# One fused two-layer attention kernel: the whole replay table (order of all queues, engines, slots, extra waits) replaced by another

## The chip, the cores and the metric

The kernel runs on one core of one Trainium2 chip. The metric is the device time of one execution in microseconds (us), the median of three runs. Five engines work in parallel, each through its own queue in order: TensorE (PE: matmuls; its weight loads are shown as PEld), VectorE (DVE), ScalarE (ACT), GpSimd (POOL) and SyncE (SP, which here only issues DMAs). ACT issues some DMAs too.

## The reference

Two layers, each an attention block A and a linear-attention block B, on x of 2048 tokens by 512 in bfloat16. Both layers use the same weights, 32 heads of 16 features.

```python
x = A_x
x = x + _A_ref(_layernorm(x), A_wq, A_wk, A_wv, A_wo, A_beta)
x = x + _B_ref(_layernorm(x), B_wqkv, B_w_phi, B_wo)
x = x + _A_ref(_layernorm(x), ...)     # the same again
x = x + _B_ref(_layernorm(x), ...)
# A: 4 segments of 512 tokens; per segment
p = softmax(q k^T * scale + causal mask);  a_dot = p v
a_mem = phi(q) M / (phi(q) z + 1e-6)       # M, z: running sums over the segments before
o = sigmoid(beta) * a_mem + (1 - sigmoid(beta)) * a_dot
M, z = M + phi(k)^T v, z + sum(phi(k))
# B: over all 2048 tokens
phi_q = [softmax(q w_phi), softmax(-q w_phi)];  phi_k the same from k
o = (phi_q (phi_k^T v)) / (phi_q sum(phi_k) + 1e-6)
```

## The kernel before

The kernel is written as a list of some 3400 small operations (`Program.add`), each with the tiles it reads and writes, the engines that may run it, and a name. It works through the four segments of layer 0 and then of layer 1. In a segment s: layernorm of its four 128-token tiles (`ln`: L801 statistics, L817 the normalised xn), a transpose of xn (on PE at the start, L601, else by a DMA transpose on SP, L585), projections to K, Q and V (`a_proj`), the scores of 32 heads in blocks (`a_att`: PE writes 128x1024 score blocks to PSUM, ACT takes their exponential into a tile PT, L1104; DVE or POOL multiplies the odd diagonal blocks by a mask into D, L1110; POOL masks the even ones in place, L1113; PE multiplies PT and D by V), normalisation, output projection and residual sum, and then the same tokens' keys and queries of block B. Almost all matmuls are recorded at one helper line, L520.

Nothing of this text decides when an operation runs. Four tables do, and `replay` turns them into queues:

- `ORDER` lists all operations by number. Each is appended in that order to the queue of its engine, so the table fixes the order in each of the five queues. A number over 10000 pairs a score block with the one in front of it, so that their matmuls alternate.
- A negative number in `ORDER` stands for idle matmuls, which multiply a tile `warm` of zeros into an unused part of a PSUM bank (L1431; -401 means 25 of them, bank 0) and give no result.
- `ENGINE` has one letter for each operation that several engines could run (a, d, p, s for ACT, DVE, POOL, SP).
- `SLOTS` says which buffer of its pool, or which PSUM banks, each tile gets. `AFTER` has pairs (x, y): operation x also waits until y is done.

```python
for n, x in enumerate(ORDER):
    if x < 0:
        f = self.idle_op((-1 - x) // 16, (-1 - x) % 16)
        ...
    self.queues[op.on].append(op.i)
...
for x, y in AFTER:
    ops[x].need.add(y)
```

`finalize` then writes each queue with the semaphore waits that the data, the reuse of slots and `AFTER` ask for. An engine whose next instruction waits does nothing else meanwhile. At the start DMAs load X (tiles 0 to 3 by single 128-token tiles of 128 KB, the other twelve by groups of four, 512 KB), the weights WA_k, WA_q, WA_v in halves of 256 KB (one half on SP, one on ACT), beta (8 KB, a copy to each partition) and, all on SP, WB_v, the raw block-B weights for k and q (into tiles EQ), WA_o and w_phi, and WB_o.

Of the kernel before, what the change touches and what calls it, by code (L numbers as in the profile page):

```python
# [33 lines left out]
    0, 20, 26, 1, 23, 21, 22, 2, 3, 24, 25, 28, 4, 5, 33, 81, 27, 6, 7, 82, 8, 9, 10, 11, 53, 16, 54, 18, 55, 60, 56, 17, 57, 12, 61, -401, 62, 63,  # L34
    29, 58, 64, 65, 59, 67, 83, 84, 66, 74, 85, 89, 34, 86, 68, 103, 69, 70, 104, 87, 30, 90, 88, 105, 115, 91, 92, 116, 75, 31, 106, 93, 96, 102,
    117, 71, 97, 94, 107, 76, 157, 95, 98, 72, 110, 158, -22, 209, 73, 177, 346, 121, 122, 210, 344, 133, 347, 178, 345, 335, -33, 166, 10161, 348,
    123, 349, 337, 162, 134, 32, 351, 108, 350, 37, 124, 163, 159, 135, 352, 99, 167, 77, 1138, 109, 130, 164, 160, 125, 338, 336, 165, 118, 1131,
    111, 339, 128, -19, 182, 1140, 340, 127, 100, 168, 183, 131, 341, 342, 112, 101, 343, 180, -83, 214, 184, 113, 119, 215, 179, 78, 404, 389, 114,
    13, 79, 185, 40, 120, 193, 10198, 14, 80, 132, 405, 45, 425, 194, 145, 136, 1129, 137, 126, 199, 148, 46, 47, 169, 138, 48, 1139, 49, 129, 146,
    406, 186, 50, 51, 354, 139, 353, 746, 181, 149, 147, 140, 52, 170, 355, 755, 142, 187, 188, 143, 356, 189, 190, 200, 171, 15, 150, 144, 172, 195,  # L40
    232, 10230, 191, 426, 359, 151, 201, 196, 753, 233, 380, 202, 152, 436, 381, 36, 231, 192, 197, 173, 174, 212, 368, 211, 382, 216, 203, 213, 175,
    204, 205, 141, 206, 217, 176, -17, 219, 218, 383, 1130, 234, 10239, 207, 1141, 371, 220, 208, 1142, 221, 240, 222, 384, 369, 1143, 223, 386, 224,
    235, 407, 747, 225, 385, 263, 242, 258, 370, 387, 264, 237, 1132, 744, 248, 357, 362, 236, 259, 388, 363, 1145, 422, 238, 249, 427, 756, 745,
    261, 423, 241, 41, 153, 424, 246, 10244, 1133, 360, 260, 372, 245, 361, 226, 748, 154, 1134, 364, 247, 250, 243, 227, 228, 251, 262, 446, 373,
    266, 437, 229, 365, 252, 374, 253, 448, 428, 377, 268, 10270, 375, 447, 449, 38, 432, 429, 450, 269, 254, 451, 430, 255, 378, 431, 453, 287, 271,
    452, 440, 438, 433, 454, 288, 366, 272, 439, 390, 19, 367, 273, 434, 290, 441, 294, 391, 376, 435, 295, 282, 749, 256, 39, 276, 283, 392, 277,
    358, 442, 754, 265, 274, 257, 393, 395, 464, 289, 275, 443, 267, 465, 379, 475, 466, 285, 396, 298, 10296, 467, 397, 408, 1135, 297, 476, 468,
    42, 472, 299, 278, 1144, 279, 43, 1136, 409, 478, 284, 1137, 469, 292, 477, 286, 306, 293, 280, 473, 479, 281, 398, 1146, 470, 307, 311, 474,
    757, 399, 758, 410, 300, 301, 312, 400, 291, 411, 483, 480, 308, 316, 413, 320, 414, 317, 760, 302, 309, 484, 481, 310, 303, 321, 415, 318, 314,
    485, 416, 319, 313, 417, 759, 322, 418, 315, 304, 324, 761, 751, 323, 325, 412, 305, 571, 420, 471, 566, 750, 419, 326, 155, 752, 401, 327, 44,  # L50
    556, 572, 328, 329, 402, 330, -33, 558, 567, 156, 403, 587, 10582, 559, 421, 588, 557, 545, 816, 574, 813, 573, 583, 546, 831, 569, 547, 562,
    10564, 584, 771, 565, 568, 772, 394, 832, 589, 563, 798, 762, 331, 590, 773, 814, 585, 774, 332, 586, 333, 815, 455, 591, 833, 614, 10619, 334,
    570, 550, 620, 763, 575, 457, 764, 780, 615, 777, 456, 458, 765, 459, 778, 460, 551, 554, 768, 641, 603, 779, 462, 548, 461, 642, 592, 795, 549,
    463, 593, 796, 555, 604, 617, 598, 797, 766, 576, 616, 594, 599, 552, 769, 577, 444, 553, 618, 595, 445, 646, 770, 639, 600, 647, 596, 781, 606,
    578, 601, 597, 579, 624, 640, 580, 637, 605, 602, 581, 486, 621, 638, 487, 607, 608, 622, 609, 775, 625, 623, 489, 610, 611, 643, 653, 10651,
    488, 648, 612, 626, 627, 654, 613, 490, 497, 628, 498, 629, 652, 807, 561, 630, 808, 644, 491, 500, 657, 10655, 631, 499, 494, 645, 492, 632,
    658, 495, 776, 493, 505, 482, 496, 501, 656, 670, 782, 671, 649, 506, 502, 650, 659, 660, 809, 1192, 503, 661, 783, 673, 665, 811, 810, 679, 507,
# [1418 lines left out]
```

## Time and profile before

| | |
|---|---|
| median of 3 runs | 480.14 us (479.97 to 481.0) |
| the profiled execution's span, first to last instruction | 479.8 us |
| mean granted TensorE clock | 1.000 |
| instructions in the profile | 19249 |
| HBM read, written | 6.32 MB, 2.10 MB |

The profiled execution's span is 0.34 us under the median. A "busy" engine in the page has an instruction in flight; matmuls overlap, and so do other engines' instructions at their edges, which is why a group's busy time is less than its count times its mean. The chain that ended last is followed back from the last instruction, at each step to what released it.

### The profile page before, as it was taken

The numbers are of one execution on the slowest core, as the hardware profiler recorded it, in microseconds if no ns is written. First come the engines' busy times: TensorE is split into PE (matmuls) and PEld (weight loads), VectorE is DVE, ScalarE is ACT, GpSimd is POOL, SyncE is SP. The second block draws the span as 40 slices with busy tenths as digits, with TensorE's granted clock in tenths as the row PEclk, the third lists the DMA queues.
The fourth block names the chain that finished last, engine by engine and source line by source line (L and its number), as shares of the span: only waits on it lengthen the run. The fifth ranks groups of instructions, "written<-read, shape, count | busy, mean of one in ns | idle before, by whom it ended". The sixth has DMA issues, their size and how long they took to land.

```text
span 479.8 us, 19249 instructions
## 1 busy us (share of the span) xinstructions
PE 464.4 (97%) x8324; PEld 320.1 (67%) x8324; DVE 428.1 (89%) x1021; ACT 430.7 (90%) x668; POOL 261.0 (54%) x420
## 2 busy tenths in 40 slices
PE   8999989999999999999999999999999999999997
PEld 7776667667856567557687666766865657665763
DVE  6999999989998988599999899999998879978785
ACT  3999999999999999986799899899999999999743
POOL 3577657646756576410246485784776578761100
PEclk9999999999999999999999999999999999999999
DMA  8978752225411232232257407236145112402376
GB/s 264 160 196 132 127 78 46 46 48 78 59 23 25 46 68 47 19 39 47 55 88 93 62 9 124 58 53 81 39 56 89 25 25 48 76 19 55 69 128 187
DMA packets 115091, 35.86 MB, mean 75 GB/s; under 512 B 106816, under 2 KB 115008, under 8 KB 115008
## 3 DMA queue, kind: packets, MB, share of 16 engines
q1 hardware_dynamic: 113184, 33.06, 39.9%
q10 hardware_dynamic: 1824, 1.58, 1.0%
q8 instruction: 65, 1.06, 0.9%
q14 instruction: 18, 0.15, 0.1%
HBM read 6.32 MB, written 2.10 MB: 18 GB/s over the span
## 4 chain that ended last, share of the span: by engine, by line
PE 40%; DVE 25%; ACT 22%; DMA 8%; POOL 3%; issue 1%; POOLq 0%; DVEq 0%
PE PS L520 38%; ACT PT L1104 16%; DVE stats L801 4%; DMA OT<-O 3%; ACT Ek L1200 3%; DVE xn L817 2%; DVE X L1165 2%; DMA EQ<-xn 2%; POOL PT L1113 2%; DVE Vt L1228 1%; DVE D L1110 1%; DMA xA<-xn 1%; DMA xB<-xn 1%; PE PS L1431 1%; DVE O L1139 1%
## 5 line engine op out<-in xcount | busy, mean ns | idle before, releaser
L1104 ACT ACTIVATE PT<-PS 128x1024 bf16<-128x1024 f32 x288 | 282.4, 1068 | 6.5 <-PE PS L520 5.6
L1110 POOL TENSOR_TENSOR D<-PT,modd 128x256 bf16<-128x256 bf16 x127 | 87.2, 697 | 41.7 <-ACT PT L1104 29.5
L1113 POOL TENSOR_SCALAR_AFFINE_SELECT PT<-PT 128x512 bf16<-128x512 bf16 x128 | 83.2, 658 | 48.1 <-DVE D L1110 43.3
L520 PEld LDWEIGHTS PS<-VT,PT 128*128 128x128 bf16 x2048 | 74.7, 96 | 18.7 <-POOL PT L1113 3.8
L520 PE MATMUL PS<-VT,PT 128*128 128x17 bf16 x2048 | 81.7, 171 | 1.5 <-POOL PT L1113 0.6
L520 PE MATMUL PS<-QT,K 32*128 32x64 bf16 (+2 forms) x2176 | 74.8, 213 | 1.1 <-ACT PT L1104 0.6
L520 PE MATMUL PS<-VT,D 128*128 128x17 bf16 x512 | 59.8, 170 | 0.0
L520 PEld LDWEIGHTS PS<-QT,K 32*128 32x128 bf16 x2176 | 40.4, 93 | 20.3 <-ACT PT L1104 10.0
L1110 DVE TENSOR_TENSOR D<-PT,modd 128x256 bf16<-128x256 bf16 x129 | 45.1, 364 | 2.1 <-ACT PT L1104 2.0
L520 PEld LDWEIGHTS PS<-VT,D 128*128 128x128 bf16 x512 | 43.2, 96 | 0.0
L1228 DVE TENSOR_TENSOR Vt<-PS,Zk 128x1024 bf16<-128x1024 f32 (+1 forms) x34 | 38.9, 1159 | 1.1 <-ACT Zk L1216 0.6
L801 DVE BATCH_NORM_STATS2 stats<-X 128x6 f32<-128x512 bf16 x56 | 37.6, 683 | 1.1 <-DMA X<-in_A_x_dram 0.7
L1200 ACT ACTIVATE Ek<-PS 128x512 bf16<-128x512 f32 x64 | 36.8, 648 | 1.6 <-PE PS L520 1.4
L1207 POOL TENSOR_TENSOR Vt<-Ek 128x512 f32<-128x512 bf16 x24 | 28.2, 1175 | 17.4 <-ACT Ek L1200 15.1
L520 PE MATMUL PS<-WA_k,xA 128*128 128x256 bf16 x256 | 36.6, 273 | 0.8 <-DVE xA L907 0.5
L1165 DVE TENSOR_TENSOR X<-X,PS 128x512 bf16<-128x512 bf16 x50 | 33.5, 678 | 4.3 <-PE PS L520 4.0
L1304 POOL COPY O<-rho 128x512 bf16<-128x512 bf16 x26 | 16.2, 642 | 38.7 <-DVE rho L1297 35.4
L520 PE MATMUL PS<-xA,WA_q 128*128 128x128 bf16 x512 | 36.4, 219 | 0.7 <-DMA xA<-xn 0.5
L520 PE MATMUL PS<-WA_v,xA 128*128 128x256 bf16 x256 | 36.3, 273 | 0.3 <-DMA xA<-xn 0.3
L520 PE MATMUL PS<-WA_o,OT 128*128 128x512 bf16 x128 | 32.1, 380 | 1.3 <-DMA OT<-O 0.7
L520 PEld LDWEIGHTS PS<-xA,WA_q 128*128 128x128 bf16 x512 | 30.0, 98 | 4.8 <-issue 1.0
L817 DVE TENSOR_SCALAR xn<-X,mv,rstd 128x512 bf16<-128x512 bf16 x64 | 28.6, 466 | 4.1 <-POOL rstd L813 1.7
(158 smaller groups left out, 983.5 us busy)
## 6 DMA issues: line engine op xcount, KB each, us to landing
X<-in_A_x_dram SPq DMA_DIRECT2D x3, 512.0 KB, 11.7
out_dram<-X SPq DMA_DIRECT2D x12, 128.0 KB, 1.8
EQ<-in_B_wqkv_dram SPq DMA_DIRECT2D x2, 512.0 KB, 4.9
OT<-O SPq DMA_TRANSPOSE x42, 3.2
WB_v<-in_B_wqkv_dram SPq DMA_DIRECT2D x1, 512.0 KB, 10.9
WA_o<-in_A_wo_dram SPq DMA_DIRECT2D x1, 512.0 KB, 4.1
WB_o<-in_B_wo_dram SPq DMA_DIRECT2D x1, 512.0 KB, 4.9
out_dram<-X ACTq DMA_DIRECT2D x4, 128.0 KB, 2.3
```

The source lines that it names most:

```text
L520: return e.matmul(o, l, r, start=st, stop=sp, tile_position=(basep(l), basep(o)))
L801: self.dve(lambda e, t=t, src=src: e.bn_stats(self.stats[:, t, :], src()), 0.603, [held() if held else R("X", t)], [R("stats", t)], name=" ...
L817: self.dve(lambda e, t=t, n=n, xn=xn: e.tensor_scalar(xn.ap[:, n], self.X[:, t, :], self.mv[:, t, 0:1], self.rstd[:, t:t + 1], op0=ALU.sub ...
L1104: self.act(lambda e, st=st, pt=pt: e.activation(pt.ap[:].rearrange("p b c -> p (b c)"), self.ps[:, st.slot[0] * 512:st.slot[0] * 512 + 102 ...
L1110: self.either(lambda e, d=d, k=k, pt=pt: e.tensor_tensor(d.ap[:, :, k, :].rearrange("p b (z c) -> p b z c", z=2), self.ends(pt.ap[:, :, 25 ...
L1113: self.pool(lambda e, q=quarters: e.affine_select(q(), q(), [[0, 4], [1, 128]], ALU.is_ge, 0.0, base=0, channel_multiplier=-1), 0.6, [pt() ...
L1139: self.dve(lambda e, r1=r1, view=view, nt=nt, g=g, o=o[ts]: e.tensor_tensor(o.ap[:, 0:nt, g, :].rearrange("p i (h d) -> p i h d", d=DH), v ...
L1165: self.dve(lambda e: e.tensor_tensor(X[:, t, :], X[:, t, :], self.bank(gen), ALU.add), 0.6, [R("X", t), gen()], [R("X", t)], name="resid")
L1200: self.act(lambda e, sgn=sgn, Ek=Ek, gen=gen: e.activation(Ek.ap[:, sgn, :], self.bank(gen), ACT.Exp, scale=1.0 - 2.0 * sgn), 512, [gen()] ...
L1207: self.pool(lambda e, Ek=Ek, sums=sums: e.tensor_tensor(sums(), *(Ek.ap[:].rearrange("p s (h j) -> p s h j", h=H)[:, :, :, 8 * k:8 * k + 8 ...
L1228: self.dve(lambda e, w=w, n=n, Vt=Vt, Zk=Zk, gen2=gen2: e.tensor_tensor(self.signed(Vt)[:, w, :, 0:16], self.bank(gen2).rearrange("p (h d) ...
L1304: P.add(("act", "pool"), {"act": lambda e, dst=dst, src=src: e.activation(dst(), src(), ACT.Copy), "pool": lambda e, dst=dst, src=src: e.t ...
```

## The change

All four tables are replaced. The operations, their sizes, their data and all code are the same; the file is ten lines longer, so L520 is now L530, L1104 is L1114 and so on.

- `ORDER`: another order in every queue. The idle matmuls were 144 in 37 places; they are 26 in two (the 25 at the start, and one).
- `ENGINE`: 234 operations run on another engine than before. In the sum by kind:

| operation | before | after |
|---|---|---|
| odd masks (D, L1110) | DVE 129, POOL 127 | DVE 151, POOL 105 |
| copies of k to ktok (L579) | ACT 16, DVE 12 | ACT 11, DVE 17 |
| copies K to KP | ACT 5, DVE 13, POOL 14 | ACT 3, DVE 18, POOL 11 |
| copies of PE transposes (xA, xB, EQ, OT) | ACT 10, DVE 14 | ACT 4, DVE 20 |
| copies of sums to X | ACT 9, DVE 5 | ACT 12, DVE 2 |
| output stores (DMA issues) | ACT 4, SP 12 | ACT 11, SP 5 |
| semaphore waits in the queues of PE, ACT, DVE, POOL, SP | 877, 517, 780, 429, 105 | 809, 493, 800, 411, 105 |
| all compute instructions on DVE, ACT, POOL | 1021, 667, 416 | 1057, 662, 385 |

- `SLOTS`: other buffers and banks. `AFTER`: 253 pairs where there were 119.

```diff
 ORDER = (
-    0, 20, 26, 1, 23, 21, 22, 2, 3, 24, 25, 28, 4, 5, 33, 81, 27, 6, 7, 82, 8, 9, 10, 11, 53, 16, ...
+    20, -401, 0, 11, 21, 8, 22, 81, 4, 6, 10, 2, 1, 82, 26, 24, 5, 25, 33, 3, 18, 7, 53, 14, 9, ...
...
 AFTER = (
-    (102, 75), (184, 112), (389, 179), (186, 49), ...
+    (24, 20), (25, 81), (26, 81), (27, 60), (31, 49), ...
```

Three places in the queues, with the numbers of the buffers. The first is SP's queue from the start of the program, which holds DMA issues alone. X of 128x512 is one token tile, of 128x4x512 four of them; EQ0, EQ1 and EQ3 here receive the raw weights of block B. Before:

```order
L587 DMA X<-in_A_x_dram 128x512
L587 DMA WA_k<-in_A_wk_dram 128x2x512
L587 DMA X<-in_A_x_dram 128x512
L587 DMA WA_q<-in_A_wq_dram 128x2x512
L587 DMA WA_v<-in_A_wv_dram 128x2x512
L587 DMA X<-in_A_x_dram 128x4x512
L587 DMA WB_v<-in_B_wqkv_dram 128x4x512
L587 DMA X<-in_A_x_dram 128x4x512 x2
L587 DMA wphi<-in_B_w_phi_dram 128x4x16
L585 DMA_TRANSPOSE xA1<-xn1 128x8x128
L585 DMA_TRANSPOSE K0<-ktok0 128x8x128
```

After, the first twelve rows:

```order
L597 DMA X<-in_A_x_dram 128x4x512
L597 DMA X<-in_A_x_dram 128x512 x2
L597 DMA WA_k<-in_A_wk_dram 128x2x512
L597 DMA X<-in_A_x_dram 128x4x512
L597 DMA WA_q<-in_A_wq_dram 128x2x512
L597 DMA EQ1<-in_B_wqkv_dram 128x4x512
L597 DMA WA_v<-in_A_wv_dram 128x2x512
L597 DMA wphi<-in_B_w_phi_dram 128x4x16
L597 DMA WA_o<-in_A_wo_dram 128x4x512
L597 DMA EQ3<-in_B_wqkv_dram 128x4x512
L597 DMA WB_v<-in_B_wqkv_dram 128x4x512
L595 DMA_TRANSPOSE OT2<-EQ3 128x8x128
```

Tiles 4 to 7 of X now go ahead of tile 1, tiles 12 to 15 ahead of the SP half of WA_q, and the raw weights ahead of WA_v. Behind the last row come the other load of X, two more transposes OT0<-EQ3 and OT1<-EQ1, and only then K0<-ktok0 and the two xA1<-xn.

The second is ACT's queue at the same place: its DMA issues and what follows up to the first exponential of scores (PT). Before:

```order
L587 DMA WA_k<-in_A_wk_dram 128x2x512
L587 DMA X<-in_A_x_dram 128x512
L587 DMA WA_q<-in_A_wq_dram 128x2x512
L587 DMA WA_v<-in_A_wv_dram 128x2x512
L587 DMA beta<-in_A_beta_dram 128x32
L483 ACT_TABLE_LOAD
```

After:

```order
L597 DMA WA_v<-in_A_wv_dram 128x2x512
L597 DMA X<-in_A_x_dram 128x512
L597 DMA WA_q<-in_A_wq_dram 128x2x512
L597 DMA beta<-in_A_beta_dram 128x32
L597 DMA WA_k<-in_A_wk_dram 128x2x512
L493 ACT_TABLE_LOAD
```

In front of both stands tile 0 of X. WA_k's ACT half has changed places with WA_v's and is now the last of ACT's loads, behind beta. Between the table load and the first exponential of scores stand 8 instructions before and 12 after: two exponentials of beta, one copy inside xA and one copy into K are the four that were added.

The third is PE's queue where block B of layer 1 ends (Rkv is its key-value sum, O its output, WB_o its output weights; L601 transposes O). Before:

```order
L520 MATMUL PS<-Rkv,PT 128x136 x32
L601 MATMUL PS<-ident,O 128x128 x4
L1431 MATMUL PS<-warm 128x240 x9
L601 MATMUL PS<-ident,O 128x128 x4
L1431 MATMUL PS<-warm 128x240 x2
L520 MATMUL PS<-Rkv,EQ 128x136 x16
L520 MATMUL PS<-WB_o,OT 128x512 x8
L1431 MATMUL PS<-warm 128x240 x4
```

After:

```order
L530 MATMUL PS<-Rkv,PT 128x136 x32
L611 MATMUL PS<-ident,O 128x128 x8
L530 MATMUL PS<-Rkv,EQ 128x136 x16
L530 MATMUL PS<-WB_o,OT 128x512 x8
L530 MATMUL PS<-Rkv,K 128x136 x16
```

The real matmuls stand in the same order there; the idle ones are gone.

More of the change, by code (lines that the diff above doesn't have):

```diff
@@ L192 @@
+    "aaaadaas"
 )
 SLOTS = (
[L194 to L197 removed]
@@ new lines @@
+    "14063034030522151801302210233101310006014205332004100425470920011051201203022303613030034011502013400112201357210328013202211609103500312223"
+    "01021000100172001300800032141360309120110521204823760120042600172200311304000120300105020122014132057023100301212017006712071041501203101132"
+    "41543313220013003121301260104017042600122211705062013002273011180721114102202603913100401001310151101200001302301012120837121311251600103220"
+    "03911223108101150192712011504053262203004001130205210521004182000022002111111010200810103705252411052100601142100040352031309112312100342321"
@@ new lines @@
+    "51700001131210221000102361401113203030202332830129131010040211103119011030603100100221021303201291001301000113180120020140302020201200045609"
+    "21100210307100131381021121310512101332140201022000031221370011523511082104160201022901200315340123011316015004052480050133240092201120010090"
+    "01315226034201053210831320111102031030021002609101203034071353203020231100020021130300190322106150331322210257113411301418323336104130102171"
+    "20003200131201039260500074083255253102321071021002200213003111310180512716901200564141114350030323122311200514310300511002132203102130232310"
@@ L207 @@
+    "0033020267322023102311010234531240713"
 )
```

26 lines of the change are left out of this document (8 added, 18 removed), and 308 rows, old and new, of tables (AFTER, ORDER).

## The prediction

> **What bounds the kernel now.** I read the page's busy shares and its chain first, then the table of 12-us stretches, since a share over the whole span mixes stages.
>
> ```profile
> PE 464.4 (97%) x8324; PEld 320.1 (67%) x8324; DVE 428.1 (89%) x1021; ACT 430.7 (90%) x668; POOL 261.0 (54%) x420
> ...
> PE 40%; DVE 25%; ACT 22%; DMA 8%; POOL 3%; issue 1%; POOLq 0%; DVEq 0%
> ```
>
> Three engines are near their limit at once, and the chain changes hands between them: no single queue carries the span. The stretches (length, then PE, PEld, DVE, ACT, POOL busy with counts, clock, DMA share, GB/s) say where.
>
> ```profile
> 0.00:12.00 12.00, 10.33 (x104) 8.51 (x105) 8.29 (x25) 4.34 (x8) 4.70 (x20) 1.00 0.83 265
> ...
> 24.00:36.00 12.00, 11.25 (x253) 9.46 (x251) 11.82 (x38) 11.04 (x19) 9.44 (x16) 1.00 0.78 196
> ...
> 72.00:84.00 12.00, 11.94 (x264) 9.12 (x262) 11.90 (x29) 11.70 (x16) 8.59 (x15) 1.00 0.24 46
> ...
> 156.00:168.00 12.00, 11.92 (x193) 6.85 (x189) 11.49 (x26) 12.00 (x18) 6.42 (x10) 1.00 0.24 46
> ...
> 456.00:468.00 12.00, 12.00 (x112) 8.02 (x111) 9.83 (x16) 4.82 (x21) 0.00 (x0) 1.00 0.70 126
> ```
>
> In the first 12 us ACT works 4.34 and loads run at 265 GB/s; in the body PE, DVE and ACT are each busy 11 to 12 us of 12; near the end ACT has little to do and PE is full. So a new order can gain little in the body except by taking work away from the three full engines, and time lost at the start, where they wait for data, is not made up later by idle engines. The opening is the stage to look at first.
>
> ```profile
> 1.04 5.18 PE L1431 MATMUL PS<-warm 128*128 128x240 bf16 x25 [1.04 <-DVE warm L702]
> ...
> 6.02 0.63 PE L601 MATMUL PS<-ident,xn 128*128 128x128 bf16 x4
> ...
> 7.61 1.07 PE L520 MATMUL PS<-xA,WA_k 128*128 128x128 bf16 x16
> ...
> 10.28 1.95 PE L520 MATMUL PS<-xA,WA_q 128*128 128x128 bf16 x32
> ...
> 12.16 0.40 PE L520 MATMUL PS<-QT,K 32*128 32x128 bf16 x8
> ...
> 12.82 3.79 ACT L1104 ACTIVATE PT<-PS 128x1024 bf16<-128x1024 f32 x4
> ```
>
> (Start, duration, engine.) 25 idle matmuls, the first transpose of xn, the first k projection at 7.61, q at 10.28, the first scores at 12.16, and from 12.82 ACT has exponentials. When the loads were issued and how long after issue they landed:
>
> ```profile
> 1.25 0.46 ACTq L587 DMA_DIRECT2D WA_k<-in_A_wk_dram  x1
> ...
> 2.22 0.43 SPq L587 DMA_DIRECT2D WA_q<-in_A_wq_dram  x1
> ...
> 2.75 0.49 ACTq L587 DMA_DIRECT2D WA_v<-in_A_wv_dram  x1
> ...
> 3.21 0.47 SPq L587 DMA_DIRECT2D X<-in_A_x_dram  x1
> 3.27 0.55 ACTq L587 DMA_DIRECT2D beta<-in_A_beta_dram  x1
> ...
> 3.73 0.58 SPq L587 DMA_DIRECT2D WB_v<-in_B_wqkv_dram  x1
> ...
> 7.14 4.96 SPq L587 DMA_DIRECT2D wphi<-in_B_w_phi_dram  x1
> ```
>
> ```profile
> WB_v<-in_B_wqkv_dram SPq DMA_DIRECT2D x1, 512.0 KB, 10.9
> ...
> WA_k<-in_A_wk_dram ACTq DMA_DIRECT2D x1, 256.0 KB, 4.1
> WA_q<-in_A_wq_dram SPq DMA_DIRECT2D x1, 256.0 KB, 6.2
> ...
> WA_v<-in_A_wv_dram ACTq DMA_DIRECT2D x1, 256.0 KB, 7.2
> ...
> beta<-in_A_beta_dram ACTq DMA_DIRECT2D x1, 8.0 KB, 8.9
> wphi<-in_B_w_phi_dram SPq DMA_DIRECT2D x1, 16.0 KB, 10.5
> ```
>
> ```profile
> X<-in_A_x_dram SPq DMA_DIRECT2D x1, 512.0 KB, 10.0
> ```
>
> (The last answer is for the stretch 3.2 to 3.3 us alone.) Issue plus landing gives a curve of bytes over time. Up to WA_k both queues have taken 768 KB: 1.25 + 4.1 = 5.35 us. Up to WA_q 1536 KB: 2.22 + 6.2 = 8.42. Up to WA_v 2048 KB: 2.75 + 7.2 = 9.95. Beta, 8 KB behind that: 3.27 + 8.9 = 12.17. On SP alone, with ACT's 1032 KB beside: 1536 KB at 3.21 + 10.0 = 13.21, 2048 KB at 3.73 + 10.9 = 14.63, 3088 KB at 7.14 + 10.5 = 17.64. I read this as two queues that share the bytes about equally and serve their own loads in order.
>
> **The opening's loads (term 1: +3.6, less 1.3).** Tile 1 of X stood first on SP; now 512 KB stand before it. 640 KB on its queue and as much on the other make 1280 KB, between 768 at 5.35 and 1536 at 8.42: 7.4 us. WA_k's two halves now end behind 1024 KB on SP and 1032 KB on ACT, so not before the 9.95 at which 2048 KB had landed; behind beta it can be as late as 12.17. That moves the first k projection from 7.61 to 10.0 at least, 12.2 at most (k work, 10.28 - 7.61 = 2.7 us, then ends at 12.7 to 14.9). WA_q's SP half ends behind 1792 KB on SP, halfway from 13.21 to 14.63: 13.9. PE serves in order, so q starts at 13.9 instead of 10.28: +3.6 (ends +2.9 and +4.6, the latter if k starts at 12.2). Scores and the first exponential follow q as before, at about 16.4. Not all is lost: ACT does four more instructions in that wait that it does later now. At 0.29 to 0.63 us each (rows of beta's exponential and of a copy, below) these are 1.2 to 2.5; I take 1.3, since DVE, which also fills its wait, gains nothing for ACT. Net +2.3, ends +0.4 and +3.4.
>
> ```profile
> 16.43 0.29 ACT L726 ACTIVATE rd<-beta 128x32 f32<-128x32 bf16 x1
> ...
> 16.79 1.33 SPq L585 DMA_TRANSPOSE xA<-xn  x1
> ```
>
> ```profile
> 16.79 5.36 DMA xA<-xn
> ```
>
> **SP's queue behind the loads (term 2: +1.0).** Three transposes of raw weights now stand ahead of K0 and xA1, and the first waits for EQ3, 3600 KB deep on SP. 3088 KB landed at 17.64 and the 1040 KB before that took 17.64 - 14.63 = 3.0, so EQ3 lands near 19.1. With 1.33 us for each issue, a load between them and K0 ahead too, xA1's first issue comes near 25, 8 us after its 16.79. It then needs 5.36 by the chain: landed near 30, where it was 22.15. PE and ACT have in front of it all projections of the first segment and nine score blocks, which themselves start 3.6 later, so most of the 8 us is covered by queued work. What is behind the waiters: PE's v projection of the next segment blocks scores; ACT's copy inside xA blocks exponentials. I price it between 0 and 8 - 3.6 = 4.4, and take 1.0, near the covered end, because nine exponentials with as many copies fill ACT from 16.4 to nearly 29.
>
> **Work moved between engines (term 3: DVE +1.5, ACT -1.0).**
>
> ```profile
> L1110 POOL TENSOR_TENSOR D<-PT,modd 128x256 bf16<-128x256 bf16 x127 | 87.2, 697 | 41.7 <-ACT PT L1104 29.5 <-PE PS L520 4.9 <-DVE PhiQ L961 2.4
> ...
> L1110 DVE TENSOR_TENSOR D<-PT,modd 128x256 bf16<-128x256 bf16 x129 | 45.1, 364 | 2.1 <-ACT PT L1104 2.0
> ...
> L579 ACT ACTIVATE ktok<-PS 128x512 bf16<-128x512 f32 x16 | 10.1, 628 | 1.3 <-PE PS L520 1.2
> ...
> L579 DVE CAST ktok<-PS 128x512 bf16<-128x512 f32 x12 | 8.1, 678 | 2.3 <-PE PS L520 2.3
> ...
> L938 DVE COPY KP<-K 128x512 bf16<-128x512 bf16 x13 | 4.1, 316 | 0.2 <-PE PS L520 0.2
> ```
>
> ```profile
> L1110 DVE TENSOR_TENSOR D<-PT,modd x129: 222/284/1245, 17.9 to 428.9; 128x256 bf16<-128x256 bf16 x129
> ```
>
> DVE gets 36 instructions: 22 masks at 45.1/129 = 0.35 us, 5 ktok copies at 8.1/12 = 0.68, and nine others net, put at KP's 0.32: 7.7 + 3.4 + 2.8 = 13.9 us. POOL loses 22 masks of 0.69 and some copies: 15 us and more of its 261. The tile's row (min/median/max 222/284/1245) says that masks on DVE are stretched at times. Were all 151 at the median they took 42.9, less than the 45.1 of 129 now. So DVE gets from -2.2 + 6.2 = +4.0 to +13.9; I take 9, since POOL stays half busy. DVE is idle 479.8 - 428.1 = 51.7 us; only where it fills its stretch (24 to 36: 11.82 of 12) does more work lengthen it. I count a sixth, +1.5 (ends 0 and +9). ACT loses 5 copies of 10.1/16 = 0.63, 3.2 us, its other moves cancelling in number; of these a third shows, as ACT is the full engine in about a third of the chain's turns: -1.0 (ends -3.2 and 0). The stores moved to ACT's queue cost nothing: near the end ACT works 4.82 of 12.
>
> [...]
>
> **Idle matmuls (term 4: -1.0).**
>
> ```profile
> 209.41 1.39 PE L1431 MATMUL PS<-warm 128*128 128x240 bf16 x12
> ```
>
> Twelve started within 1.39 us, so one takes (1.39 - 0.27) / 11 = 0.10 us; 118 fewer free 12 us of PE. Nearly all of it was time in which PE waited for ACT or DVE, and it will wait still. What shows is where real matmuls stood ready behind them, somewhere between 0 and 12; I take 1, the length of one such burst, as few bursts are on the chain.
>
> **The sum.** +2.3 + 1.0 + 1.5 - 1.0 - 1.0 = +2.8 on a span of 479.8: 482.6. The end stage is costed at nothing, since DVE, PE and ACT have the same instructions left behind the last exponential to within two, idle matmuls and store issues apart. So are `AFTER`'s 134 more pairs: the queues hold 90 fewer waits in all, so most pairs name what is waited for anyway. The median stands 0.34 over the span: 482.9. A fifth of a per cent, 1 us, is about what this measurement can tell from no change.
>
> **Rivals.** The first ends on the other side: the new order gives back more by hiding DMA transposes.
>
> ```profile
> 65.32 5.30 DMA OT<-O
> ...
> 211.27 5.06 DMA OT<-O
> ...
> 325.58 5.01 DMA EQ<-xn
> ```
>
> The chain crosses such transposes at 5 us each, 8% of 479.8 = 38 us in all. If the new order lays other work under them, PE's idle 479.8 - 464.4 = 15.4 and the 12 us of idle matmuls are what can be had; a third of these 27 is 9, against the +2.8 + 1.0 (term 4 is in it) of the rest: 480.1 + 3.8 - 9 = 475. It decides from 4 us on. For it speaks the chain's 38 us, against it that DVE and ACT are full in the same stretches and DVE gets more. Chance 0.33.
>
> The second: PE loses its clock in the opening. The 25 idle matmuls took 5.18 us, 0.2 each, twice the 0.10 of later ones, though the granted clock reads 1.00 throughout: PE starts at half pace and is at full pace by 7.61 (16 matmuls in 1.07). After the change the idle matmuls still end near 6.2, and xn of tile 0 stands on DVE behind the statistics of tile 1, which wait for 7.4; PE is then idle until about 9 and, but for two transposes, until 10 to 12. If the pace falls back, the following stream runs at half for as long as it did from 1.04 to 6.2, and loses up to half of 5.2: 482.9 + 2.6 = 485.5. Chance 0.18. [...]
>
> The third: the opening's delay is swallowed, because segment 1's exponentials waited anyway, and nothing else moves: within 1 us of 480.1. Chance 0.13.
>
> **How the numbers follow.** Forecast, 481.1 to 484.5: 0.36. Clock rival, 484.5 to 487: 0.18. No change: 0.13. Faster: 0.33. So slower 0.54, same 0.13, faster 0.33. The range runs from the faster rival's 475 to 487.5 (the upper ends of terms 1 and 2 without the clock, or the clock rival with its own); the forecast's own range is 481.1 to 484.5.
>
> **What the changed profile would show.** First k projection after 10 us, q near 14, the first L1114 near 16.4 (each under 13.5 would refute term 1). WA_k and WA_q landing last of what PE waits for. xA1's transpose issued after 22 us, with an ACT or PE wait on it near 29. DVE busy 432 to 442, ACT near 428, POOL near 243. The matmuls of the k projection at 0.06 us apart or at twice that decide the clock rival. PE's busy share should fall to 93 or 94% as the idle matmuls go. I would be wrong if loads in one queue do not wait for those in front, or if the body closes up by more than 4 us.

## The result, and the profile after

The changed kernel takes 477.77 us against 480.25 beside it: a ratio of 0.9945 (95% interval 0.993 to 0.996), so 2.5 us faster, where 482.9 and slower was forecast. (One of its four executions was disturbed and took 1265 us; the comparison leaves it out.) The profiled execution's span is 475.2 us, 4.6 less than before, and its time 476.92. The profiled pair shows more than the medians do: other executions of the kernel before, beside the runs below, have spans of 477.3 to 480.3, in the median 478.6, so that the profiled 479.8 is one of its longest, while 476.92 is the changed kernel's shortest time. First the page of the changed kernel, busy shares and chain.

```profile
PE 455.1 (96%) x8206; PEld 314.1 (66%) x8206; DVE 420.1 (88%) x1057; ACT 427.7 (90%) x663; POOL 241.8 (51%) x389
...
PE 53%; ACT 31%; DVE 12%; DMA 2%; issue 1%; POOL 1%; SPq 0%
```

DVE is busy 8.0 us less than before (428.1), although it has 36 instructions more. ACT's 427.7 and POOL's 241.8 are as forecast. DMA has gone from 8% of the chain to 2%, and DVE from 25% to 12%. The same five stretches as in the prediction (length, then PE, PEld, DVE, ACT, POOL, clock, DMA, GB/s):

```profile
0.00:12.00 12.00, 5.97 (x33) 4.06 (x34) 6.66 (x22) 2.19 (x3) 3.03 (x13) 0.93 0.82 263
...
24.00:36.00 12.00, 12.00 (x235) 10.36 (x233) 11.96 (x39) 11.97 (x20) 8.83 (x16) 1.00 0.77 132
...
72.00:84.00 12.00, 11.79 (x264) 8.94 (x262) 11.93 (x34) 11.73 (x17) 7.88 (x13) 1.00 0.24 46
...
156.00:168.00 12.00, 11.93 (x210) 6.79 (x206) 10.90 (x20) 12.00 (x19) 9.12 (x16) 1.00 0.15 25
...
456.00:468.00 12.00, 11.55 (x92) 6.72 (x91) 9.11 (x17) 4.01 (x17) 0.00 (x0) 1.00 0.73 165
```

The first row has lost: ACT 2.19 instead of 4.34. The second has gained: ACT 11.97 instead of 11.04. Where the time goes is best seen at the starts of the exponentials of scores (L1104, L1114), counted from 0 to 287; us from the start of the span, read from the trace:

| exponential | 0 | 12 | 120 | 144 | 192 | 252 | 287 | end |
|---|---|---|---|---|---|---|---|---|
| before | 12.8 | 33.9 | 171.3 | 238.8 | 309.5 | 384.7 | 432.2 | 479.8 |
| after | 19.8 | 37.5 | 172.0 | 238.8 | 308.6 | 379.9 | 427.7 | 475.2 |
| difference | +7.0 | +3.6 | +0.7 | 0.0 | -0.9 | -4.8 | -4.5 | -4.6 |

The opening loses 7.0 us, of which 3.6 are left at exponential 12. From there the body (12 to 287) takes 390.2 us instead of 398.3, 8.1 less, most of it in two parts: up to 120 (2.9), and from 192 to 252 in layer 1 (3.9). By the medians the body gains less, some 6 us (2.5 in all and the opening's 3.6). The end stage is unchanged. The opening on PE after:

```profile
8.07 0.40 PE L611 MATMUL PS<-ident,xn 128*128 128x128 bf16 x4 [1.85 <-DVE xn L827]
...
12.03 3.57 PE L530 MATMUL PS<-xA,WA_k 128*128 128x128 bf16 x32 [2.69 <-DVE rstd L821]
...
17.34 1.95 PE L530 MATMUL PS<-xA,WA_q 128*128 128x128 bf16 x32
19.22 0.40 PE L530 MATMUL PS<-QT,K 32*128 32x128 bf16 x8
```

The row at 12.03 names DVE's rstd as what ended the wait, but that was done at 11.56. WA_k's ACT half, issued at 3.42, took 8.5 us and landed at 11.94:

```profile
WA_k<-in_A_wk_dram ACTq DMA_DIRECT2D x1, 256.0 KB, 8.5
```

Then PE does the 32 k matmuls in 3.57 us, 0.11 each, where 16 took 1.07 us before, 0.07 each, and q, which stands behind the rest of the k work, comes at 17.34. On SP after (issue start, length):

```profile
18.64 1.41 SPq L595 DMA_TRANSPOSE OT<-EQ  x1
...
24.17 1.32 SPq L595 DMA_TRANSPOSE K<-ktok  x1
26.29 1.49 SPq L595 DMA_TRANSPOSE xA<-xn  x1
```

The transposes of raw weights (OT<-EQ) do stand in front of K0 and xA1, which is issued at 26.29 instead of 16.79. The granted clock was 1.00 throughout before; now it falls to half twice before the last microsecond, from 10.3 to 17.1 us and here (clock in the third column from the right):

```profile
167.31:170.73 3.42, 2.83 (x111) 2.43 (x109) 2.94 (x10) 3.42 (x6) 2.24 (x4) 1.00 0.11 25
170.73:177.55 6.82, 6.82 (x126) 4.10 (x124) 4.65 (x14) 5.86 (x9) 4.48 (x7) 0.50 0.17 32
```

### The profile page after: what moved, and what is told of

It reads as the page before. It is cut to its first block, busy times and chain, and to the rows that moved or that the text cites. A ratio compares the mean times of both kernels' runs of the same rounds, so it can differ in the third digit from the quotient of the medians.

```text
span 475.2 us, 18978 instructions
## 1 busy us (share of the span) xinstructions
PE 455.1 (96%) x8206; PEld 314.1 (66%) x8206; DVE 420.1 (88%) x1057; ACT 427.7 (90%) x663; POOL 241.8 (51%) x389
## 4 chain that ended last, share of the span: by engine, by line
PE 53%; ACT 31%; DVE 12%; DMA 2%; issue 1%; POOL 1%; SPq 0%
PE PS L530 52%; ACT PT L1114 22%; ACT Ek L1210 3%; DVE Vt L1238 1%; DMA X<-in_A_x_dram 1%; DVE stats L811 1%; DMA OT<-O 1%; DVE X L1175 1%; PE PS L611 1%; ACT K L1295 1%; ACT phi L969 1%; ACT EQ L1295 1%; ACT QT L589 1%; DVE O L1149 1%; DVE O L1352 1%
## 5 line engine op out<-in xcount | busy, mean ns | idle before, releaser
L1114 ACT ACTIVATE PT<-PS 128x1024 bf16<-128x1024 f32 x288 | 281.0, 1059 | 5.6 <-PE PS L530 4.3
L1123 POOL TENSOR_SCALAR_AFFINE_SELECT PT<-PT 128x512 bf16<-128x512 bf16 x128 | 83.5, 662 | 55.4 <-DVE D L1120 33.4
L1120 POOL TENSOR_TENSOR D<-PT,modd 128x256 bf16<-128x256 bf16 x105 | 71.6, 692 | 45.0 <-DVE D L1120 7.8
L530 PEld LDWEIGHTS PS<-VT,PT 128*128 128x128 bf16 x2048 | 74.5, 96 | 17.0 <-POOL PT L1123 3.5
L530 PE MATMUL PS<-VT,PT 128*128 128x17 bf16 x2048 | 81.3, 171 | 1.3 <-DVE O L1149 0.6
L530 PE MATMUL PS<-QT,K 32*128 32x64 bf16 (+2 forms) x2176 | 74.2, 214 | 1.1 <-ACT PT L1114 0.4
L530 PE MATMUL PS<-VT,D 128*128 128x17 bf16 x512 | 59.9, 171 | 0.0
L530 PEld LDWEIGHTS PS<-QT,K 32*128 32x128 bf16 x2176 | 40.2, 93 | 17.3 <-ACT PT L1114 8.2
L530 PEld LDWEIGHTS PS<-VT,D 128*128 128x128 bf16 x512 | 43.3, 96 | 0.0
L811 DVE BATCH_NORM_STATS2 stats<-X 128x6 f32<-128x512 bf16 x56 | 37.5, 683 | 3.3 <-DMA X<-in_A_x_dram 3.0
L1217 POOL TENSOR_TENSOR Vt<-Ek 128x512 f32<-128x512 bf16 x24 | 28.3, 1178 | 19.0 <-ACT Ek L1210 15.0
L530 PE MATMUL PS<-WA_v,xA 128*128 128x256 bf16 x256 | 35.7, 273 | 0.3 <-ACT phi L969 0.3
L530 PE MATMUL PS<-xA,WA_q 128*128 128x128 bf16 x512 | 35.6, 219 | 0.2 <-DVE PhiQ L971 0.2
L530 PE MATMUL PS<-WA_k,xA 128*128 128x256 bf16 x256 | 35.3, 278 | 0.1
L530 PE MATMUL PS<-WB_o,OT 128*128 128x512 bf16 x128 | 32.5, 380 | 0.5 <-DMA OT<-O 0.4
L530 PEld LDWEIGHTS PS<-xA,WA_q 128*128 128x128 bf16 x512 | 29.5, 98 | 4.7 <-issue 1.5
L530 PE MATMUL PS<-WA_o,OT 128*128 128x512 bf16 x128 | 31.8, 380 | 0.3 <-DVE OT L589 0.2
```

What stands on the lines that cost most here:

```text
L530: return e.matmul(o, l, r, start=st, stop=sp, tile_position=(basep(l), basep(o)))
L811: self.dve(lambda e, t=t, src=src: e.bn_stats(self.stats[:, t, :], src()), 0.603, [held() if held else R("X", t)], [R("stats", t)], name=" ...
L1114: self.act(lambda e, st=st, pt=pt: e.activation(pt.ap[:].rearrange("p b c -> p (b c)"), self.ps[:, st.slot[0] * 512:st.slot[0] * 512 + 102 ...
L1120: self.either(lambda e, d=d, k=k, pt=pt: e.tensor_tensor(d.ap[:, :, k, :].rearrange("p b (z c) -> p b z c", z=2), self.ends(pt.ap[:, :, 25 ...
L1123: self.pool(lambda e, q=quarters: e.affine_select(q(), q(), [[0, 4], [1, 128]], ALU.is_ge, 0.0, base=0, channel_multiplier=-1), 0.6, [pt() ...
L1217: self.pool(lambda e, Ek=Ek, sums=sums: e.tensor_tensor(sums(), *(Ek.ap[:].rearrange("p s (h j) -> p s h j", h=H)[:, :, :, 8 * k:8 * k + 8 ...
```

## The experiments

Times are medians; "ratio" is to the kernel before in the same job, which was 479.8 to 480.7. Exponentials are named by number as above.

### The opening: which part of its delay is paid at the end

The kernel h_open0 takes the opening from the kernel before and all else from the changed one (the other three tables follow):

```diff
-ORDER = changed kernel's
+ORDER = first 78 entries of the kernel before (up to the first score block), then the changed kernel's without these
```

> The changed kernel with the opening of the kernel before: its loads, projections and everything else up to the first score block stand in the old order, all behind that in the new. First exponential near 12.8 us again instead of 19.8. Theory 1 (PE and ACT are full from there on, so the delay is carried to the end): 470 to 471.5. Theory 2 (transposes on SP and the loads limit the first segments, so most is swallowed): 475 to 478, the first exponentials earlier but the second segment's at the same time as in the changed kernel.

480.11 us, ratio 0.9988 (0.9974 to 1.0002): slower than the changed kernel, with a faster start. Its first exponential is at 13.1, but exponential 12 at 39.4, later than the changed kernel's 37.5. The waits between 18 and 40 us (in all, times, longest):

```profile
...
ACT xA L918 <- DMA xA<-xn: 4.3, 1, 4.3
...
PE PS L530 <- DMA xA<-xn: 3.8, 1, 3.8
```

PE and ACT wait for xA1. (The clock is also at half here from 15.15 to 18.56 and from 28.81 to 35.64, and in the next run it is not, so the difference between the two includes this.) In the old order of loads EQ is among the last, SP waits for it at OT<-EQ until 21.4, and xA1 stands behind. So one more row is put back:

```diff
 SP:
+K0<-ktok0, xA1<-xn1 x2
 OT2<-EQ3, OT0<-EQ3, OT1<-EQ1
-K0<-ktok0, xA1<-xn1 x2
```

> h_open0 with one move: on SP's queue the three transposes OT<-EQ of the raw weights stand behind K0<-ktok0 and the two xA1<-xn instead of ahead of them. Theory 1 (in h_open0 those transposes, which waited for EQ until 21.4 us, kept xA1 and so PE and ACT waiting): xA1's issue falls from 26.9 to 17 to 19 us, the twelfth exponential comes from 39.4 to 31 to 34, and 5 to 7 us are carried to the end: 473 to 475. Theory 2 (the body swallows it, its later transposes set the pace): 478 to 480, with the twelfth exponential early and the thirty-sixth near 69 as in h_open0.

```profile
16.85 1.58 SPq L595 DMA_TRANSPOSE K<-ktok  x1
20.75 2.87 SPq L595 DMA_TRANSPOSE xA<-xn  x2
```

K0 is issued at 16.85 and xA1 at 20.75; exponential 12 comes at 33.4, 4.1 before the changed kernel, and the lead stands at 3.9 at the end: 473.44 us, ratio 0.9852 (0.9834 to 0.9871). Next to nothing of it is swallowed. The opening as changed costs 477.77 - 473.44 = 4.3 us, and this hybrid beats both kernels. The fourth combination (a_T) has the new loads with that same move on SP:

> The changed kernel with its own loads, but with the three transposes of raw weights behind K0<-ktok0 and the two xA1<-xn on SP, the move that turned 480.1 into 473.4 with the old loads. Theory 1 (loads and transposes cover each other: with q at 17.3 and the first exponential near 19 the second segment's data is not waited for, since xA1 can't be issued before xn at 21 to 22): 476.5 to 478. Theory 2 (the transposes alone cost 4 us): 473 to 474.5.

476.19 us, ratio 0.9911 (0.9898 to 0.9925): 1.6 less than the changed kernel. So the move is worth 6.7 with the old loads and 1.6 with the new ones, a little more than theory 1 allowed: by the times, the late loads cover most of the late transposes. The trace does not show where the 1.6 are made: the profiled execution of a_T is its slowest (478.29), with exponential 12 at 38.3 and the clock at half once more, from 39.14.

a_wopen fills PE's wait in the opening:

```diff
 ORDER (PE's queue)
+12 idle matmuls
 transpose of xn
+4 idle matmuls
 transpose of xn
+22 idle matmuls
 k projection
```

> The changed kernel with 38 idle matmuls more in the opening: 12 ahead of the first transpose of xn on PE, 4 between the two, 22 behind the second, in the time in which PE waited for data. Theory 1 (the fall of the clock at 10.3 us delays the first exponential but not the second segment, which waits for xA1's transpose): the k projection at twice the pace, the first exponential at 16.5 to 18 instead of 19.8, exponential 12 still at 37 to 38, the whole 477 to 478.5. Theory 2 (the delay is carried to the end, the rival's price): 474.5 to 476.

The clock stays: from the first k matmul to the first of q it is 2.88 us instead of 5.31. The first exponential comes at 17.1 instead of 19.8, and exponential 12 at 37.8, no earlier. What holds it up is xA1, which lands at 31.1; from 12 to 45 us the waits show

```profile
ACT xA L918 <- DMA xA<-xn: 2.7, 1, 2.7
```

where those of the changed kernel, from 15 to 45 us, name no DMA. So the fall in the opening costs up to 2.7 us at the first exponential (0.3 of it comes from a k that starts sooner) and nothing at exponential 12, since SP's queue sets that. But the whole takes 485.27, ratio 1.0114 (1.0074 to 1.0154), which neither theory said: in the profiled execution, the fastest of its four, another 4.4 us are lost from exponential 48 on, with the same queues, but for the idle matmuls, as the changed kernel. In that trace 13 of 49 transposes of the body take over 4 us from issue to landing, where the changed kernel has 4; why these were slow stays open.

### The idle matmuls and the clock

```diff
-ORDER (kernel before) with 144 idle matmuls
+ORDER with the 25 at the start
```

> The kernel before, its tables unchanged but for the 119 idle matmuls behind the opening, which are taken out of ORDER (the 25 at the start stay). Theory 1 (PE is the bound of the body, and idle matmuls stand in front of real ones that are ready): 119 x 0.10 = 12 us of PE go, of which a third to two thirds shows: 472 to 476, near or under the changed kernel's 477.8. Theory 2 (the prediction's term 4, they fill waits for ACT and DVE): 479 to 480. Theory 3 (they hold up the granted clock): stretches at 0.5 appear where PE pauses, and the time rises over 480.

486.2 us, ratio 1.0123 (1.0095 to 1.0152). Up to exponential 120 it stays within 0.3 us of the kernel before: the idle matmuls there cost nothing. Then the clock falls three times, at 171.1, 362.25 and 403.21; the first two:

```profile
167.69:171.10 3.41, 2.42 (x104) 2.08 (x108) 2.69 (x9) 3.41 (x5) 2.16 (x3) 1.00 0.40 76
171.10:177.90 6.80, 5.94 (x111) 3.39 (x107) 4.49 (x15) 5.15 (x8) 4.61 (x8) 0.50 0.21 41
358.80:362.25 3.45, 1.95 (x71) 1.39 (x68) 2.40 (x11) 3.45 (x5) 2.34 (x4) 1.00 0.36 69
362.25:365.66 3.41, 3.18 (x65) 2.25 (x65) 3.34 (x9) 2.73 (x4) 1.65 (x3) 0.50 0.19 38
```

In the 3.4 us ahead of these PE was busy 2.42 and 1.95 us, and yet the clock went. Against the kernel before the exponentials slip by 1.9, 0.9 and 2.3 us at the three falls and regain 1.9 elsewhere. Theory 3 holds. The changed kernel, which also lacks them, falls once in the body, at 170.7. a_w170 was to mend that:

```diff
 ORDER (changed kernel)
 score block 119
+7 idle matmuls, bank 0
...
+4 idle matmuls, bank 4
 score block 120
```

> The changed kernel with 11 idle matmuls more on PE: 7 behind score block 119, where PE waited 0.59 us, and 4 in front of score block 120. Nothing else is moved. Theory 1 (the granted clock falls at 170.7 because the 3.4 us before hold only matmuls of 32 rows or of 8 to 17 columns; the share of rows times columns is 0.22 there and 0.41 or more everywhere in the kernel before): no clock fall near 170, exponential 132 is 1.4 us earlier against exponential 120, and the end 1.0 to 2.0 earlier: 475.8 to 476.8. Theory 2 (the fall has another cause, or its cost is swallowed by the layer's end): 477.5 to 478.

479.72, ratio 0.9996 (0.9977 to 1.0015), 2 slower than the changed kernel. The 7 waited 1.60 us for the exponential that still read their bank, since the kernel lets idle matmuls wait for what used their bank before, and PE waited with them; the clock fell all the same, now for 3.4 us. It tells nothing of the clock's price. In "best" they stand in a part of PSUM that nobody reads at that time:

```diff
 ORDER (h_open0T)
+7 idle matmuls, upper half of bank 7
 product of PT and V, op 1331
```

> h_open0T with 7 idle matmuls more, in the free half of PSUM bank 7, in front of the last product of probabilities and V ahead of 168 us, so that they wait for nothing. They raise the share of rows times columns in the 3.4 us around it from 0.18 to 0.39. Theory 1 (a share over a third keeps the clock): no clock fall at 167, 0.7 to 2.0 us less than h_open0T: 471.5 to 472.8. Theory 2 (the 0.7 us that they take on PE cost as much): 473 to 474.

No fall in the body of its profile, and exponentials 120 to 132 take 17.7 us instead of 19.6, so this fall costs about 1.9. 473.12 us, ratio 0.9846 (0.9831 to 0.9861): the lowest median of all, but its interval overlaps h_open0T's, so a gain over that is not shown; two of its other executions have a mean clock under 1 (0.996 and 0.993).

### Is the body's gain bound to a stage, or to the engines?

h_b_a has the kernel before up to the first score block of layer 1 and the changed one behind it, h_a_b the reverse (the other tables follow):

```diff
-ORDER = one kernel's
+ORDER = first 1741 entries of the kernel before, then the changed kernel's rest    (h_b_a)
+ORDER = first 1726 entries of the changed kernel, then the other's rest    (h_a_b)
```

> A hybrid: the tables of the kernel before up to the first score block of layer 1 (exponential 144, which starts at 238.8 us in both traces), those of the changed kernel behind it. Theory 1 (the gain is made in layer 1 alone and hangs on its own order): 477 to 478, as the changed kernel. Theory 2 (the order of layer 0 prepares it, by what is already done at the boundary): 479 to 482.

> The opposite hybrid: the changed kernel's tables up to the first score block of layer 1, the kernel before behind it. Theory 1 (layer 1 makes the gain by itself): 480 to 481, as the kernel before. Theory 2 (layer 0 prepares it): 477 to 479.

483.47, ratio 1.0073 (1.0055 to 1.0092), and 485.0, ratio 1.0091 (1.0069 to 1.0113): both slower than either parent, so the totals answer neither theory. The seam costs: h_b_a loses 3.2 us between exponentials 144 and 156. Stage by stage they answer: against the kernel before, h_b_a gains 3.9 from 192 to 252, as the changed kernel does there, and h_a_b, up to 120 in the changed tables, has its lag fall from 3.4 at exponential 12 to 1.0. But h_a_b also gains 1.3 from 192 to 252, where it has the tables of the kernel before: the profiled execution of that kernel was slow there by about as much, and some 2.6 of the 3.9 are the tables'. With this taken off, each stage's gain goes with the tables of that stage.

The next two exchange ENGINE alone:

```diff
-ENGINE = "..." of the kernel itself
+ENGINE = "..." of the other kernel
```

> The changed kernel with the ENGINE letters of the kernel before: 22 masks back on POOL, 5 ktok copies back on ACT and so on; its order, slots and waits stay. Theory 1 (the order makes the gain, the letters are worth the 3 us of ACT work they take off and cost nothing on DVE): 479 to 481.5. Theory 2 (the prediction's term 3, DVE's addition costs as much as ACT's relief brings): 477 to 478.5. Theory 3 (the letters make the whole gain): 482 to 485.

> The kernel before with the ENGINE letters of the changed one; its order, slots and waits stay. Theory 1 (the letters are worth ACT's 3 us at most): 478 to 480. Theory 2 (term 3: +0.5): 480 to 481.5. Theory 3 (the letters make the whole gain): 475 to 477. An order laid out for other engines may also lose by it: over 482.

501.16, ratio 1.043 (1.0411 to 1.0448), and 502.22, ratio 1.0447 (1.0424 to 1.0471). 20 us are lost in both directions, which no theory priced; only the last sentence on b_engA named such a loss. Letters, order and waits are one plan here, and exchanging the letters alone does not price them.

### DMA transposes

By the traces, 12 of 52 transposes of xn and O landed less than 0.5 us before PE used them in the kernel before, 4 of 52 in the changed one; but 47 and 46 had less than 3 us. First the transposes behind the opening are delayed:

```diff
+DMA_TRANSPOSE spare<-WA_k 128x512, waiting for what the next row waits for
 DMA_TRANSPOSE of xn or O      (65 times)
```

> The kernel before; in front of each DMA transpose of xn and O in the body (from the second segment of layer 0 on) SP issues a second one of 128x512, of WA_k into a spare tile, that waits for the same data. It gives no result and makes each of these transposes land later by its issue, about 1.2 us, and by its share of the transfer, up to 3 in all. Theory 1 (the kernel before waits for such transposes: its chain crosses six of them behind 45 us): + 6 x 1.2 to 3, so 487 to 498. Theory 2 (they are hidden, and the chain only names one of several that end together): 481 to 485.

> The changed kernel with the same second transposes in front of its own. Theory 1 (the new order hides transposes: its chain crosses one behind 45 us, at 452): half of what the kernel before loses or less, 479 to 485. Theory 2 (the gain has nothing to do with transposes): the same loss as in the kernel before, within 2 us.

520.77 (ratio 1.0853, 1.082 to 1.0885) and 535.08 (ratio 1.1144, 1.1123 to 1.1165). The changed kernel loses more, 57 us against 40. So its order does not lay more work under its transposes. Part of the loss is the clock, whose mean is 0.952 (a_dT) and 0.970 (b_dT) in the two profiled executions. Then the tiles are made sooner, by plain copies, which leave out the transposing, so that the values are no attention any more:

```diff
-dma_start(dst, src, transpose=True)
+dma_start(dst, src)      (xn and O, from the second segment on)
```

> The kernel before with its DMA transposes of xn and O in the body (from the second segment of layer 0 on) replaced by plain DMA copies of the same tiles, so the values are no attention any more; a copy's issue should take about 0.5 us instead of 1.24 and it should land 1 to 2 us sooner. Theory 1 (the kernel before loses its 8 us to waits for transposes: 12 of 52 have under 0.5 us to spare): its stretch from exponential 12 to the last, 398.3 us, shrinks by 5 to 9, and the whole to 471 to 475. Theory 2 (the 8 us are lost elsewhere): it shrinks by 0 to 3, to 477 to 480.

> The changed kernel with the same replacement of its transposes by plain copies. Theory 1 (its transposes land in time, 4 of 52 under 0.5 us): its stretch from exponential 12 to the last, 390.2 us, shrinks by 0 to 3, so that the gap of 8.1 between the two falls under 4. Theory 2: both shrink alike and the gap stays at 6 to 9.

478.48 (0.9972, 0.9962 to 0.9981) and 475.49 (0.9919, 0.9892 to 0.9947). The DMA rows of before, and of b_cp:

```profile
OT<-O SPq DMA_TRANSPOSE x42, 3.2
```

```profile
OT<-O SPq DMA_DIRECT2D x41, 256.0 KB, 2.3
```

Landing 0.9 us sooner shortens the kernel before's body from 398.3 to 395.8. The changed kernel's goes from 390.2 to 389.2, 0.8 of it from a shorter fall of the clock. The gap falls from 8.1 to 6.6, not under 4. So landing 0.9 us sooner closes 1.5 of the gap; what landing sooner still would close is not shown.

### The extra waits

All pairs of AFTER, 119 before and 253 after, let a POOL instruction wait for a DVE instruction. They can be left out:

```diff
-AFTER = ((24, 20), (25, 81), ...)
+AFTER = ()
```

> The changed kernel with an empty AFTER: the 253 extra waits are gone, everything else stays. Theory 1 (the prediction's cost of nothing: most name what is waited for anyway): 477 to 479. Theory 2 (they hold transposes and loads back so that these don't collide, and so make part of the gain): 480 to 485. Theory 3 (they cost waits): 474 to 476.5.

> The kernel before with an empty AFTER: its 119 waits of POOL for DVE are gone. Theory 1 (they keep POOL from an instruction that would stretch DVE's): DVE's instructions on SBUF that overlap with POOL, 458 ns in the mean before, rise to 480 or more, and the time by 3 to 8: 483 to 488. Theory 2 (order alone makes the difference): within 1 us of 480.

487.97, ratio 1.0175 (1.0143 to 1.0206), and 485.44, ratio 1.0106 (1.0075 to 1.0137). The body (exponential 12 to 287) of the kernel before, of the changed one, and of both with AFTER empty (b_noafter, a_noafter), in this order; in each row length, PE, PEld, DVE, ACT, POOL:

```profile
33.90:432.20 398.30, 389.23 (x7381) 267.51 (x7380) 363.98 (x872) 377.78 (x547) 238.40 (x370) 1.00 0.37 58
```

```profile
37.50:427.70 390.20, 382.57 (x7322) 263.52 (x7321) 357.58 (x908) 376.50 (x547) 219.71 (x341) 0.99 0.35 58
```

```profile
34.50:435.00 400.50, 389.81 (x7381) 267.78 (x7379) 368.55 (x872) 378.64 (x548) 239.13 (x370) 1.00 0.36 58
```

```profile
37.40:438.70 401.30, 384.22 (x7322) 263.94 (x7321) 371.96 (x908) 378.43 (x547) 220.17 (x342) 0.99 0.34 56
```

Without the waits the changed kernel's body is 0.8 us longer than the other's (401.3 and 400.5); with them 8.1 shorter. (These lengths hold to a microsecond or so: b_noafter's profiled execution, 484.21, is its fastest, a_noafter's, 489.05, one of its slower two.) They take 14.4 us off DVE's busy time in the changed kernel (371.96 to 357.58) and 4.6 in the kernel before (368.55 to 363.98), while ACT's moves by 2 at most. What gets shorter is seen at DVE's groups, those of xn in the kernel before, the changed one and a_noafter, with the masks D of the last two:

```profile
L817 DVE TENSOR_SCALAR xn<-X,mv,rstd 128x512 bf16<-128x512 bf16 x64 | 28.6, 466 | 4.1 <-POOL rstd L813 1.7 <-ACT rstd L808 1.6 <-DMA xA<-xn 0.3
```

```profile
L1120 DVE TENSOR_TENSOR D<-PT,modd 128x256 bf16<-128x256 bf16 x151 | 45.7, 319 | 1.5 <-ACT PT L1114 0.8 <-PE PS L530 0.2
...
L827 DVE TENSOR_SCALAR xn<-X,mv,rstd 128x512 bf16<-128x512 bf16 x64 | 25.1, 412 | 3.1 <-POOL rstd L823 1.4 <-ACT rstd L818 1.2
```

```profile
L1097 DVE TENSOR_TENSOR D<-PT,modd 128x256 bf16<-128x256 bf16 x151 | 47.7, 331 | 1.4 <-ACT PT L1091 0.8 <-PE PS L507 0.3
...
L804 DVE TENSOR_SCALAR xn<-X,mv,rstd 128x512 bf16<-128x512 bf16 x64 | 29.7, 483 | 3.4 <-POOL rstd L800 1.8 <-ACT rstd L795 1.4
```

xn takes 412 ns in the mean, 466 before, 483 without waits. Over all DVE instructions that read SBUF alone (masks, xn, PhiK, PhiQ, KP, xA, MSb), those that overlap a POOL instruction for over a tenth of their time last 380 ns in the changed kernel and 454 in a_noafter, 458 in the kernel before and 494 in b_noafter; those that don't, 315 to 332 in all four. The masks alone show the same: 360 and 398, 425 and 481 ns with POOL beside, 276 to 279 without. It is not the number of those that overlap that falls (176 of 348 in the changed kernel, 174 in a_noafter) but the time: they overlap for 47.2 us in all with the waits and for 61.5 without.

Are more such waits enough? b_more adds 87 to the kernel before, each where its trace showed a DVE instruction that met POOL and lasted longer than its median (88 of them, 28.3 us over their medians in all):

```diff
 AFTER = (kernel before: 119 pairs)
+87 pairs (POOL instruction, DVE instruction that met it and lasted longer than its median)
```

> The kernel before, its order, letters and slots unchanged, with 87 more pairs in AFTER: each lets a POOL instruction wait for the DVE instruction that it had stretched in the trace (88 instructions, 28.3 us over their medians, 26.1 of it covered). Theory 1 (the body's 8 us are those of more such waits): the mean of DVE's overlapped instructions falls from 458 ns to under 400, as in the changed kernel (380), and the time to 472 to 477. Theory 2 (POOL's later masks hold up PE as much, unless the order is laid out for it): 479 to 485, with the mean lower but PE waiting for POOL.

493.97, ratio 1.0285 (1.0253 to 1.0316). Fewer DVE instructions meet POOL (155 instead of 185), and the sum over those that read SBUF alone falls from 130.1 to 123.9 us; but the mean of those that do meet it is 449 ns, not under 400 as theory 1 had it. PE pays, as theory 2 said, and by more than it allowed. Weight loads waiting for POOL's masks, in the kernel before and in b_more:

```profile
PEld PS L520 <- POOL PT L1113: 3.8, 11, 0.6
```

```profile
PEld PS L528 <- POOL PT L1121: 12.1, 23, 1.5
```

So more such waits do not pay in any order; that the changed order pays for its waits because it gives POOL the time is likely, but not shown.

## Why the prediction was wrong

**The step that failed** is the sentence in the sum that costed AFTER's 134 more pairs at nothing, "since the queues hold 90 fewer waits in all, so most pairs name what is waited for anyway". All pairs are of one kind, POOL behind DVE, which the numbers of the table would have told, and a count of waits does not price a pair. Emptying the table costs 10.2 us in the changed kernel (487.97 - 477.77) and 4.8 in the kernel before (485.44 - 480.69), so the difference is worth -5.4; by the ratios it is 11.0, 5.1 and -5.9, and the intervals leave some 2 us either way. A part of the 10.2 goes by the clock: the body of a_noafter's trace has a second fall, at 408.94. With both tables empty the change is 487.97 - 485.44 = +2.5 us, or +3.3 by the ratios; the sum forecast +2.8. That the sum of everything but these waits came about right is partly luck, as the terms show:

- *Term 1, the loads.* The place and the direction were right: WA_k was last, PE idle until 12.03 (forecast 10.0 to 12.2). The first exponential came 7.0 later instead of 3.6, because the k work ran at half pace (0.11 us a matmul, the granted clock at 0.50 from 10.30 to 17.13) and q stood behind it: WA_q had landed at 13.13 (forecast 13.9), and q began at 17.34. That is what the clock rival named, which was held to be a case apart; ahead of the fall, from 6.89 to 10.30, PE was busy 0.79 of 3.41 us. Yet a_wopen shows that nothing of that pace reaches exponential 12. By the times, the new loads alone cost 2.8 (a_T against h_open0T); forecast 2.3.
- *Term 2, SP's queue.* EQ3 was forecast near 19.1 and landed at 18.63, xA1 near 25 and issued at 26.29. The wait for it near 29 did not come: ACT had work, since the first exponential was so late. The move on SP's queue is worth 1.6 behind the new loads; forecast 1.0. Terms 1 and 2 together were +3.3 net; taking both back gave 4.3 (h_open0T). That the two cover each other was right in kind: the move is worth 6.7 with the old loads.
- *Term 3, the engines.* ACT's 428 and POOL's 243 came as 427.7 and 241.8. DVE was forecast at 432 to 442 and had 420.1; with AFTER empty its page shows 434.7. The added work was sized right, and the waits took it off again. (ACT's 3.2 us were scaled by "a third of the chain's turns", where the row gives ACT 22%; that moves the sum by 0.3.) No run shows the +1.5 by itself, since the letters exchanged alone lose 20 us; that a half-busy POOL speaks for 9 us out of 4.0 to 13.9 was the author's estimate. What the runs show in its place is the overlap: DVE's instructions on SBUF last 458 ns with POOL beside and 332 without in the kernel before, and those with POOL beside 380 in the changed kernel and 454 with AFTER empty. The waits, which shorten them, decided the sign.
- *Term 4, idle matmuls.* Forecast -1.0 for taking them out; b_noidle shows +5.9 in the kernel before, and in its trace each slip stands at a fall of the clock. The changed kernel, almost without them, has one fall in its body, of some 1.9 us. PE's share was to fall to 93 or 94% and is 96%, because the span fell too.
- *The faster rival* gave 475 by 9 us from transposes in the body. The size was near (8.1 in the profiled pair, some 6 by the medians), the mechanism hardly: 1.5 of the 8.1 goes when transposes land 0.9 us sooner. DMA's share of the chain, 8% to 2%, told where the chain passed, not what sooner transposes would give.
- *The body "closes up by more than 4 us"* was named as what would make the prediction wrong, and did.

What stays open: what of the order gives POOL the time that its 253 waits take; whether the waits pay by DVE's shorter instructions alone or also by when POOL's own work is done; and why some transposes take 4 to 5 us.

## What to carry to other kernels

A table of extra waits is a part of the schedule: look up which engines its pairs join before costing it at nothing, and compare an instruction's mean with its median and its overlap with the other engine. An edit to letters, order or waits of a replayed plan is priced only together with the others, since letters or waits alone lost up to 20 us here. A share of the chain is no price: delay the suspect and make it sooner, and see what the span does.

## What the hardware showed unexpectedly

- In the traces of this case the falls of the clock go with little work in the array and not with little busy time of PE. Stretches at half last 3.41 us (h_open0, from 15.15) and 6.83 (the changed kernel, from 10.30 and from 170.73), so cut each trace into windows of 3.41 us from there. Add up rows times columns of the matmuls in each, as a share of 128 rows and 2.4 columns per ns, the pace of idle matmuls (240 columns every 0.10 us). Of 46 falls in the runs of this case, 44 follow a window of at most 0.35; of 2365 windows that kept the clock, 2 lie under 0.33. In the changed kernel the falls at 10.30 and 170.73 and the one in the last microsecond follow 0.13, 0.22 and 0.19, and the windows that kept the clock have 0.39 or more; in the kernel before, without a fall, all have 0.41 or more. PE's busy share does not sort them: a window with 0.93 went before a fall (b_noidle, at 403.21), one with 0.48 kept the clock (a_dT, from 35.37). At 167.31 in the changed kernel PE was busy 2.83 of 3.42 us, and the share was 0.22: matmuls of 32 rows, or of 8 to 17 columns. (By a change it is tested in three runs: a_wopen and best, which add idle matmuls, have no fall in the stretch that these fill, and b_noidle, which takes them out, has three.)
- A DMA transpose issued behind 30 us with no other DMA in flight or issued in the next 2.5 us took 3.06 us to land, in the median, in both kernels (27 and 18 such). Company goes with slow ones: over 4 us took 10 of 66 with it and none of 27 without in the changed kernel, 27 of 77 and 4 of 18 in the kernel before. So company is not all of it.
